# Router gates computed from logits that travel with the gathered token rows, and GpSimd's queue in program order

## The chip, the cores and the metric

The kernel runs on one core of one Trainium2 chip. The metric is the time of one execution in device microseconds. An engine is named PE (TensorE matmuls), PEld (TensorE weight loads), DVE (VectorE), ACT (ScalarE), POOL (GpSimd) or SP (SyncE, which here only issues DMAs).

## What is computed

Three stages run one after another on 3072 tokens of 384 numbers. The first is a complex decaying linear attention, the second a dense gated product, the third a mixture of 8 experts in which each token goes to one expert. The change touches the seam between the second and the third, and the third.

```python
def _moe_ref(x, w_a, w_b, w_out):
    return (x @ w_a) * (x @ w_b) @ w_out

def _moe2_ref(x, w_gate, w1, w2):              # x is [3072, 384], 8 experts
    logits = x @ w_gate
    expert_idx = np.argmax(logits, axis=1)
    logits_shift = logits - logits.max(-1, keepdims=True)
    probs = np.exp(logits_shift)
    probs /= probs.sum(-1, keepdims=True) + 1e-09
    gate_w = probs[np.arange(N), expert_idx]
    for e in range(E):
        mask = expert_idx == e
        h = np.maximum(x[mask] @ w1[e], 0.0)
        out[mask] = gate_w[mask, None] * (h @ w2[e])
```

Because the chosen expert is the one with the largest logit, its gate is 1 divided by the sum of the exponentials of the shifted logits.

## The kernel before

The tokens go through attention and the dense stage in 12 blocks of 256 (j = 0 to 11, two chunks of 128 each). Up to the end of block 10 the order of all instructions on all engines is written out by a planner (`Plan`, with costs and due times). The dense stage of block 11 and the whole expert stage are put together by `merge`, which interleaves lists of steps by position. In that part ACT keeps the order in which the program names its instructions; the order on the other engines, POOL among them, is chosen by the framework's scheduler from its own estimate of times.

At the end of a block's dense stage the PSUM tile `o` of a chunk holds 384 numbers of the token vector and, behind them, 8 router logits (392 columns). `close` copies the 384 into `x2`, and SP stores `x2` to the DRAM table `x2d`. `close` also copies the 8 logits to `lgt`. `route` finds each token's expert from `lgt` (`pick`), its place in that expert's list (`count`, `place`), and scatters the token's number into the table `idtab` (`scatter`, POOL, line 663). `pick` leaves the shifted logits in the resident tile `sh`.

`gates` is called twice: for blocks 0 to 10 while block 11 is in the dense stage, and for block 11 during the first expert slot. It takes the exponential of `sh` on ACT (line 672), sums, adds 1e-9 and inverts on DVE (lines 674 to 676), transposes on PE, and stores one number per token to the DRAM table `gated`.

The expert stage has ten slots, in this order: (0,0), (1,0), (0,BT), (1,BT), then experts 2 to 7. The first four hold 256 tokens each, the others between 372 and 448, in chunks of up to 128 rows. Experts 2, 3 and 4 have a last chunk of 64, 48 or 32 rows of another form. A slot runs through eight steps `up(f)` (nine matmuls into a PSUM tile `h_p`, of which there are two; ACT's Relu at line 780 makes `hH` from it, DVE at line 782 the remainder `hL`) and, two steps behind, `down(f)` (matmuls into `o`, line 803). After the last `up` the next slot's rows are transposed (`turn`, lines 748 to 750). After the last `down` ACT or DVE multiplies `o` by the gate into `ye` (lines 813, 811), and POOL scatters `ye` to the output (line 814).

`fetch` for the slot two later is placed at 0.6 to 0.7 of a slot. SP loads the token numbers `ids` (line 726); then POOL issues one indirect DMA per chunk for the rows `xg` from `x2d` and, behind these, one per chunk for the gates `gt` from `gated` (both line 732).

Of the kernel before, what the change touches and what calls it, by code (L numbers as in the profile page):

```python
# [21 lines left out]
TWO = 2  # L22
# [110 lines left out]
def general(tc, ra, rb, q, k, v, a_re, a_im, w_a, w_b, w_out, w_gate, w1, w2, out, xd, x2d):  # L133
# [27 lines left out]
    with tc.If(ra > 0):  # L161
# [66 lines left out]
        with ExitStack() as ctx:  # L228
# [20 lines left out]
            with tc.For_i(0, NT // C, 1) as i:  # L249
                x = p.tile([128, DM], F32, tag="x", name="g_x")  # L250
                nc.sync.dma_start(out=x, in_=xd.rearrange("(n p) c -> n p c", p=C)[i])
                _, (xH, xL) = rows(p, ps, ident, x)
                o = ps.tile([128, DM], F32, tag="o", name="g_o")
                for f in range(NF):
                    u = []
                    for nm in "ab":
                        t = ps.tile([128, C], F32, tag=nm, name="g_ab")
                        wH, wL = W[nm, f]
                        product(t, [((wH[:, kk * C:(kk + 1) * C], wL[:, kk * C:(kk + 1) * C]), (xH[:, kk], xL[:, kk])) for kk in range(3)])
                        u.append(t)  # L260
# [8 lines left out]
                nc.sync.dma_start(out=x2d[0:NT].rearrange("(n p) c -> n p c", p=C)[i], in_=x2)  # L269
    with tc.If(rb > 0):  # L270
        with ExitStack() as ctx:
# [13 lines left out]
            with tc.For_i(0, NE, 1) as e:  # L285
# [7 lines left out]
                with tc.For_i(0, NT // C, 1) as i:  # L293
                    x = p.tile([128, DM], F32, tag="x", name="g_x")
                    nc.sync.dma_start(out=x, in_=x2d[0:NT].rearrange("(n p) c -> n p c", p=C)[i])
                    xt, (xH, xL) = rows(p, ps, ident, x)
# [153 lines left out]
def body(tc, q, k, v, a_re, a_im, w_a, w_b, w_out, w_gate, w1, w2, out):  # L450
    ins = (q, k, v, a_re, a_im, w_a, w_b, w_out, w_gate, w1, w2)
    with ExitStack() as ctx:
        dram = ctx.enter_context(tc.tile_pool(name="dram", bufs=1, space=bass.MemoryType.DRAM))
        xd = dram.tile([NT, DM], F32, name="xd")
        x2d = dram.tile([NT + 1, DM], F32, name="x2d")
        ra, rb = fast(tc, *ins, out, dram, x2d)
# [4 lines left out]
def fast(tc, q, k, v, a_re, a_im, w_a, w_b, w_out, w_gate, w1, w2, out, dram, x2d):  # L461
# [5 lines left out]
    with ExitStack() as mctx, ExitStack() as ctx:  # L467
# [41 lines left out]
        nc.vector.memset(acc, 0.0)  # L509
        sh = const.tile([128, NT // C, NE], F32, name="sh")  # L510
        gate = const.tile([128, NT // C], F32, name="gate")
        tok = const.tile([128, NT // C], U32, name="tok")
        nc.gpsimd.iota(tok, pattern=[[C, NT // C]], base=0, channel_multiplier=1)
        gated = dram.tile([NT + 1, 1], F32, name="gated")
        idtab = dram.tile([NE * REG, 1], U32, name="idtab")
# [85 lines left out]
        def route(j, late):  # L601
# [3 lines left out]
            def pick():  # L605
# [4 lines left out]
                G["r"], G["oh"] = r, oh  # L610
                sj = sh[:, 2 * j:2 * j + 2]
                eb = ebias.unsqueeze(1).to_broadcast([128, 2, NE])
# [102 lines left out]
        def fetch(e, r0, pool):  # L715
# [4 lines left out]
            def f():  # L720
                ids = pool.tile([128, most], U32, tag="ids" + tag, name="ids", bufs=3)
                same = sum(r == ts[0][1] for _, r, _ in ts)
                for a, b in ((0, same), (same, len(ts))):
                    if a < b:
                        o, r, n = ts[a][0], ts[a][1], b - a
                        nc.sync.dma_start(out=ids[0:r, a:b], in_=idtab.rearrange("(e r) one -> e r one", e=NE)[who[e], r0 + o:r0 + o + n * r].rearrange("(p c) one -> p (c one)", c=n))
                xg = pool.tile([128, most, DM], F32, tag="xg" + tag, name="xg", bufs=2)
                gt = pool.tile([128, most], F32, tag="gt" + tag, name="gt", bufs=3)
                for t, src in ((xg, x2d), (gt, gated)):
                    for c, (_, r, _) in enumerate(ts):  # L730
                        o = t[0:r, c] if t is xg else t[0:r, c:c + 1]
                        nc.gpsimd.indirect_dma_start(o, None, src, bass.IndirectOffsetOnAxis(ap=ids[0:r, c:c + 1], axis=0), bounds_check=NT, oob_is_err=False)  # L732
                SL[e, r0] = [ids, xg, gt, None, None]
            return f
# [18 lines left out]
        def expert(e, r0, pool, after_up):  # L753
# [8 lines left out]
            def up(f):  # L762
                def go():
                    _, _, _, xH, xL = SL[e, r0]
                    t = p_ab.tile([128, n_], F32, tag="ab", name="h_p")
# [22 lines left out]
            def down(f, cs=range(nt)):  # L788
                def go():
# [3 lines left out]
                    for c in cs:  # L793
# [10 lines left out]
                        if f == NH - 1:  # L804
                            y = (mo.tile([128, DM], F32, tag="x2", name="ye", bufs=2) if e < TWO else pool.tile([128, DM], F32, tag="ye", name="ye", bufs=4))
                            if both:
                                nc.vector.tensor_copy(out=y[0:m], in_=G["o", c])
                                nc.gpsimd.dma_start(out=y[0:r], in_=y[r:m], accum_op=ALU.add)
                                nc.gpsimd.tensor_scalar(out=y[0:r], in0=y[0:r], scalar1=gt[0:r, c:c + 1], scalar2=None, op0=ALU.mult)
                            elif c % 2:  # L810
                                nc.vector.tensor_scalar(out=y[0:r], in0=G["o", c], scalar1=gt[0:r, c:c + 1], scalar2=None, op0=ALU.mult)
                            else:
                                nc.scalar.activation(out=y[0:r], in_=G["o", c], func=ACTF.Copy, scale=gt[0:r, c:c + 1])  # L813
                            d = nc.gpsimd.indirect_dma_start(out, bass.IndirectOffsetOnAxis(ap=ids[0:r, c:c + 1], axis=0), y[0:r], None, bounds_check=NT - 1, oob_is_err=False)  # L814
# [187 lines left out]
        def close(j, c):  # L1002

            o = G["o", j, c]
            x2 = mo.tile([128, DM], F32, tag="x2", name="x2", bufs=2)
# [439 lines left out]
        def prefill():  # L1445
            late = x2d[NT - BT:NT].rearrange("(p c) (n t) -> p (c n) t", c=2, t=C)
            fills = [(idtab.rearrange("(p c) one -> p (c one)", p=128), dum, "rx"), (x2d[NT:NT + 1, :].rearrange("a (n t) -> (a n) t", t=C), zeros[0:3, 0:C], "z"), (gated[NT:NT + 1, :], zeros[0:1, 0:1], "z"),
                     (gated[NT - BT:NT].rearrange("(a t) one -> a (t one)", a=1), zeros[0:1], "z")]
            fills += [(late[:, 2 * i:2 * i + 2].rearrange("p n t -> p (n t)"), zeros, "z") for i in range(3)]
            for n, (o, i, x) in enumerate(fills):  # L1450
# [133 lines left out]
```

## Time and profile before

| | before |
|---|---|
| median of 3 runs | 912.55 us (911.75 to 915.97) |
| the profiled execution, its own time | 914.04 us |
| its span, first to last instruction | 912.2 us |
| PE busy | 850.9 us (93%) |
| DVE, ACT, POOL busy | 557.2, 477.2, 352.5 us |

The profile is of one execution. Times in it count from the first instruction. The expert stage begins at about 645.7 us, when the last matmul of the dense stage is issued. An engine's busy share does not by itself say what an operation is worth; what the engine waited for in that stretch does. The start of a PE record is when the engine took the matmul up, and its end is modelled. A wait named "issue" ended with nothing that the profile shows.

### The profile page before, as it was taken

What the parts mean: (1) busy time and instruction counts of PE and PEld (TensorE: products, weight loads), DVE (VectorE), ACT (ScalarE), POOL (GpSimd) and SP (SyncE); (2) the same over time, 40 slices, a digit from 0 to 9 for tenths busy, and PEclk for the clock granted to TensorE, in tenths of its full rate; (3) what the DMA queues carried; (4) which work ended last, traced back from release to release, by engine and by line L of the source; (5) the groups of instructions that cost most, each with busy time, mean ns of one, the idle gap of its engine ahead of it and who ended that gap; (6) DMA issues with size and microseconds to landing.
All of it is one profiled execution on the core that took longest, in us unless ns stands there. A gap on an engine that the chain in (4) does not pass through costs nothing.

```text
span 912.2 us, 20675 instructions
## 1 busy us (share of the span) xinstructions
PE 850.9 (93%) x8188; PEld 816.7 (90%) x8188; DVE 557.2 (61%) x1217; ACT 477.2 (52%) x887; POOL 352.5 (39%) x338
## 2 busy tenths in 40 slices
PE   0399999999999999999999999999995999999995
PEld 0387899999999999999999999999995999999995
DVE  6999997683838475666757593445731545455540
ACT  6487887574656474655655552224521534344430
POOL 2341441414454545363544444204163343444311
PEclk9999999999999999999999999999997999999998
DMA  9999964433242452627274524123341544454511
GB/s 254 276 279 236 244 142 124 103 90 100 69 96 81 109 170 65 200 60 217 63 208 69 167 59 145 36 88 122 105 153 35 160 133 138 147 161 129 164 51 25
DMA packets 134379, 120.17 MB, mean 132 GB/s; under 512 B 37284, under 2 KB 128820, under 8 KB 134271
## 3 DMA queue, kind: packets, MB, share of 16 engines
q1 hardware_dynamic: 121151, 100.51, 39.3%
q0 software_dynamic: 11392, 17.43, 8.3%
q8 instruction: 67, 1.10, 0.5%
q10 hardware_dynamic: 1728, 0.79, 0.4%
q14 instruction: 41, 0.34, 0.2%
HBM read 82.42 MB, written 10.56 MB: 102 GB/s over the span
## 4 chain that ended last, share of the span: by engine, by line
PE 72%; issue 13%; DMA 5%; POOL 5%; DVE 3%; SPq 1%; ACT 0%; POOLq 0%; DVEq 0%; ACTq 0%
PE ab_p L957 31%; PE o L1000 16%; PE h_p L771 4%; PE sc_p L1335 4%; PE y_p L1374 4%; PE o L803 4%; PE ab_p L965 3%; POOL gt L732 2%; POOL out_dram L814 2%; PE o L971 2%; PE kv_p L1394 2%; DMA out_dram<-ye,ids 1%; PE kn_p L1344 1%; DMA v<-in_v_dram 1%; DMA ids<-idtab 1%
## 5 line engine op out<-in xcount | busy, mean ns | idle before, releaser
L957 PE MATMUL ab_p<-xH,wL 128*128 128x256 f32 x792 | 220.9, 279 | 0.0
L957 PEld LDWEIGHTS ab_p<-xH,wL 128*128 128x128 f32 x792 | 148.8, 188 | 0.0
L991 POOL TENSOR_TENSOR gL<-g,gH 128x256 fp32r<-128x256 f32 x96 | 80.3, 838 | 171.4 <-ACT gH L987 166.9
L980 ACT COPY g<-ab_p 128x256 f32<-128x256 f32 x132 | 48.8, 370 | 133.6 <-PE ab_p L957 124.3
L983 DVE TENSOR_TENSOR g<-g,ab_p 128x256 f32<-128x256 f32 (+1 forms) x148 | 60.7, 410 | 90.3 <-ACT g L980 87.0
L957 PE MATMUL ab_p<-xH,waH 128*128 128x256 f32 x396 | 113.7, 287 | 0.0
L957 PE MATMUL ab_p<-xL,waH 128*128 128x256 f32 x396 | 111.1, 281 | 0.0
L957 PE MATMUL ab_p<-xH,wbH 128*128 128x256 f32 x396 | 110.6, 279 | 0.0
L957 PE MATMUL ab_p<-xL,wbH 128*128 128x256 f32 x396 | 110.4, 279 | 0.0
L1000 PE MATMUL o<-woH,gH 128*128 128x392 f32 x264 | 96.4, 365 | 0.0
L1000 PE MATMUL o<-wL,gH 128*128 128x392 f32 x264 | 90.3, 342 | 0.0
L1000 PE MATMUL o<-woH,gL 128*128 128x392 f32 x264 | 90.2, 342 | 0.0
L771 PE MATMUL h_p<-sH,w1H 128*128 128x256 f32 (+5 forms) x240 | 78.2, 326 | 11.2 <-issue 10.2
L803 PE MATMUL o<-w2H,h 128*128 128x384 f32 (+3 forms) x312 | 86.2, 340 | 0.0
L771 PE MATMUL h_p<-sL,w1H 128*128 128x256 f32 (+5 forms) x240 | 77.4, 323 | 0.0
L771 PE MATMUL h_p<-sH,w1L 128*128 128x256 f32 (+5 forms) x240 | 77.4, 322 | 0.0
L987 ACT ACTIVATE gH<-g 128x256 fp32r<-128x256 f32 x132 | 54.5, 413 | 40.3 <-DVE g L983 36.7
L957 PEld LDWEIGHTS ab_p<-xH,waH 128*128 128x128 f32 x396 | 74.5, 188 | 0.9 <-issue 0.2
L957 PEld LDWEIGHTS ab_p<-xL,waH 128*128 128x128 f32 x396 | 74.6, 188 | 0.4
L957 PEld LDWEIGHTS ab_p<-xL,wbH 128*128 128x128 f32 x396 | 74.5, 188 | 0.0
L957 PEld LDWEIGHTS ab_p<-xH,wbH 128*128 128x128 f32 x396 | 74.4, 188 | 0.0
L814 POOL DMA_INDIRECT out_dram<-ye,ids x29 | 30.2, 1040 | 92.9 <-ACT ye L813 84.2
(210 smaller groups left out, 2162.8 us busy)
## 6 DMA issues: line engine op xcount, KB each, us to landing
raw<-in_moe_w_dram SPq DMA_DIRECT2D x64, 384.0 KB
q<-in_q_dram SPq DMA_DIRECT2D x24, 192.0 KB
v<-in_v_dram SPq DMA_DIRECT2D x24, 192.0 KB
raw<-in_moe_w_a_dram SPq DMA_DIRECT2D x12, 384.0 KB
raw<-in_moe_w_b_dram SPq DMA_DIRECT2D x12, 384.0 KB
raw<-in_moe_w_out_dram SPq DMA_DIRECT2D x12, 384.0 KB
wL<-a POOLq DMA_DIRECT2D x24, 192.0 KB
x2d<-x SPq DMA_DIRECT2D x24, 192.0 KB
```

The costliest lines, as they stand in the source:

```text
L771: nc.tensor.matmul(out=t, lhsT=lh[:, o:o + 128], rhs=rh[:, kk], start=n == 0, stop=n == 8)
L803: nc.tensor.matmul(out=G["o", c], lhsT=lh, rhs=rh, start=f == 0 and n == 0, stop=f == NH - 1 and n == len(ops) - 1)
L814: d = nc.gpsimd.indirect_dma_start(out, bass.IndirectOffsetOnAxis(ap=ids[0:r, c:c + 1], axis=0), y[0:r], None, bounds_check=NT - 1, oob_is ...
L957: nc.tensor.matmul(out=t[:, i], lhsT=lh[:, kk * 128:(kk + 1) * 128], rhs=rh[:, kk], start=n == 0, stop=n == 8)
L965: nc.tensor.matmul(out=t[:, i], lhsT=A32[nm, f][:, kk * 128:(kk + 1) * 128], rhs=xT["F", 0][:, kk, cs[0]:cs[0] + len(cs)].rearrange("p c t ...
L980: nc.scalar.copy(out=G["g", j, f], in_=G["ab", j, f][:, 0])
L983: nc.vector.tensor_tensor(out=G["g", j, f], in0=G["g", j, f], in1=G["ab", j, f][:, 1], op=ALU.mult)
L987: nc.scalar.activation(out=G["H", j, f], in_=G["g", j, f], func=ACTF.Copy)
L991: eng.tensor_tensor(out=G["L", j, f], in0=G["g", j, f], in1=G["H", j, f].bitcast(F32), op=ALU.subtract)
L1000: nc.tensor.matmul(out=G["o", j, c], lhsT=lh[:, c * C:(c + 1) * C], rhs=rh, start=f == first and n == 0, stop=f == last and n == 2)
L1335: nc.tensor.matmul(out=S["p", hg][:, h], lhsT=pq["k", j][:, hg * 4 + h, c, :], rhs=pq["q", j][:, hg * 4 + h, c, 0:C], start=True, stop=True)
L1374: nc.tensor.matmul(out=t[q4 * 32:q4 * 32 + 32, kk], lhsT=a, rhs=b, start=f0, stop=f1)
```

## The change

The logits are stored and gathered with the token vector: rows of `x2d` grow from 384 to 392 numbers, `close` copies all 392 columns, and `xg` holds 392 per row. The table `gated`, the tiles `sh` and `gate`, both calls of the old `gates`, and all gathers of `gt` go. In each slot, after `up(2)`, a new `gates` has ACT copy the 8 logits of each gathered row out of `xg` into `ex`, and DVE take their largest and subtract it; after `up(5)`, `gated` has ACT take the exponential and DVE sum, add 1e-9 and invert into `gt`. Slots whose last chunk has another size do this in two parts. In the part put together by `merge`, POOL too now keeps the order in which the program names its instructions.

```diff
-        x2d = dram.tile([NT + 1, DM], F32, name="x2d")
+        x2d = dram.tile([NT + 1, DM + NE], F32, name="x2d")
...
-                sj = sh[:, 2 * j:2 * j + 2]
+                sj = mo.tile([128, 2, NE], F32, tag="sj", name="sj")
...
-        def gates(t0, t1):
-
-            def f():
-                n = t1 - t0
-                ex = mo.tile([128, NT // C, NE], F32, tag="rx", name="ex")
-                nc.scalar.activation(out=ex[:, 0:n], in_=sh[:, t0:t1], func=ACTF.Exp)
-                gs = gate[:, t0:t1].unsqueeze(2)
-                nc.vector.tensor_reduce(out=gs, in_=ex[:, 0:n], axis=AX.X, op=ALU.add)
-                nc.vector.tensor_scalar(out=gs, in0=gs, scalar1=1e-9, scalar2=None, op0=ALU.add)
-                nc.vector.reciprocal(out=gs, in_=gs)
-                t = p_sc.tile([n, C], F32, tag="sc", name="gt_p")
-                nc.tensor.transpose(t, gate[:, t0:t1], ident)
-                gT = mo.tile([NT // C, C], F32, tag="gT", name="gT")
-                nc.vector.tensor_copy(out=gT[0:n], in_=t)
-                nc.sync.dma_start(out=gated[t0 * C:t1 * C].rearrange("(n t) one -> n (t one)", t=C), in_=gT[0:n])
-            return f
...
-                xg = pool.tile([128, most, DM], F32, tag="xg" + tag, name="xg", bufs=2)
-                gt = pool.tile([128, most], F32, tag="gt" + tag, name="gt", bufs=3)
-                for t, src in ((xg, x2d), (gt, gated)):
-                    for c, (_, r, _) in enumerate(ts):
-                        o = t[0:r, c] if t is xg else t[0:r, c:c + 1]
-                        nc.gpsimd.indirect_dma_start(o, None, src, ...)
+                xg = pool.tile([128, most, DM + NE], F32, tag="xg" + tag, name="xg", bufs=2)
+                for c, (_, r, _) in enumerate(ts):
+                    nc.gpsimd.indirect_dma_start(xg[0:r, c], None, x2d, ...)
...
+        def gates(e, r0, pool):
...
+                gt = S_[2] = pool.tile([128, most, 1], F32, tag="gt" + tag, name="gt", bufs=2)
+                ex = pool.tile([128, most, NE], F32, tag="ex" + tag, name="ex", bufs=1)
+                same = sum(r == ts[0][1] for _, r, _ in ts)
+                parts = [(a, b, ts[a][1]) for a, b in ((0, same), (same, len(ts))) if a < b]
+                for a, b, r in parts:
+                    nc.scalar.copy(out=ex[0:r, a:b], in_=S_[1][0:r, a:b, DM:DM + NE])
+                for a, b, r in parts:
+                    x, g = ex[0:r, a:b], gt[0:r, a:b]
+                    nc.vector.tensor_reduce(out=g, in_=x, axis=AX.X, op=ALU.max)
+                    nc.vector.tensor_tensor(out=x, in0=x, in1=g.to_broadcast([r, b - a, NE]), op=ALU.subtract)
...
+        def gated(e, r0):
...
+                for a, b, r in parts:
+                    nc.scalar.activation(out=ex[0:r, a:b], in_=ex[0:r, a:b], func=ACTF.Exp)
+                for a, b, r in parts:
+                    g = gt[0:r, a:b]
+                    nc.vector.tensor_reduce(out=g, in_=ex[0:r, a:b], axis=AX.X, op=ALU.add)
+                    nc.vector.tensor_scalar(out=g, in0=g, scalar1=1e-9, scalar2=None, op0=ALU.add)
+                    nc.vector.reciprocal(out=g, in_=g)
...
                 st.append((0.98, up(f)))
+                if f == 2:
+                    st.append((0.1, gates(e, r0, pool if e >= TWO else xp)))
+                if f == 5:
+                    st.append((0.1, gated(e, r0)))
...
-                nc.scalar.copy(out=x2, in_=o[:, 0:DM])
+                nc.scalar.copy(out=x2, in_=o)
             else:
-                nc.vector.tensor_copy(out=x2, in_=o[:, 0:DM])
+                nc.vector.tensor_copy(out=x2, in_=o)
...
-        mctx.enter_context(tc.manual_schedule(engines={mybir.EngineType.Activation}))
-        NL = 2 * (NB - 1)
+        mctx.enter_context(tc.manual_schedule(engines={mybir.EngineType.Activation, mybir.EngineType.Pool}))
...
-              (0.45, 0.5, [(1, gates(0, NL)), (1, fetch(0, 0, xp)), (1, fetch(1, 0, xp))]))
+              (0.45, 0.5, [(1, fetch(0, 0, xp)), (1, fetch(1, 0, xp))]))
...
-                st.append((0.02, 0.5, route(NB - 1, True)[0] + [(0.2, gates(NL, 2 * NB)), (0.1, check)]))
+                st.append((0.02, 0.5, route(NB - 1, True)[0] + [(0.1, check)]))
```

## Rows read from the trace of the kernel before

**Rows 1.** The page, granted TensorE clock in 40 slices, tenths of full speed.

```profile
PEclk9999999999999999999999999999997999999998
```

**Rows 2.** Windows by slot: length, busy (count) of each engine, clock, DMA share, GB/s.

```profile
682.00:712.10 30.10, 19.91 (x129) 19.70 (x128) 5.07 (x12) 5.02 (x12) 8.94 (x9) 0.83 0.12 37
...
764.30:795.00 30.70, 30.70 (x172) 29.57 (x171) 15.76 (x30) 12.45 (x23) 13.14 (x13) 1.00 0.47 146
```

**Rows 3.** Windows around trains of POOL's DMAs, columns PE, PEld, DVE, ACT, POOL.

```profile
662.80:671.30 8.50, 8.50 (x64) 8.39 (x63) 4.15 (x7) 3.58 (x7) 6.84 (x6) 1.00 0.38 129
...
684.20:694.40 10.20, 0.06 (x1) 0.06 (x1) 1.04 (x2) 0.96 (x2) 7.07 (x8) 0.71 0.23 75
694.40:698.80 4.40, 4.40 (x18) 4.40 (x19) 0.85 (x2) 0.77 (x2) 0.00 (x0) 0.50 0.02 7
...
744.70:755.40 10.70, 10.70 (x59) 10.35 (x58) 4.81 (x9) 4.57 (x7) 8.43 (x8) 1.00 0.54 172
```

**Rows 4.** Timeline of PE: start, duration, instruction, [idle before <- what ended it].

```profile
681.17 0.34 PE L803 MATMUL o<-w2H,hL 128*128 128x384 f32 x1
...
683.87 0.28 PE L771 MATMUL h_p<-sH,w1L 128*128 128x256 f32 x1
694.35 0.58 PE L771 MATMUL h_p<-sH,w1H 128*128 128x256 f32 x1 [10.19 <-issue]
...
711.17 0.33 PE L803 MATMUL o<-w2H,hL 128*128 128x384 f32 x1
...
730.78 0.34 PE L803 MATMUL o<-w2H,hL 128*128 128x384 f32 x1
...
736.25 0.45 PE L771 MATMUL h_p<-sH,w1H 128*128 128x448 f32 x1 [0.97 <-DVE h L784]
```

**Rows 5.** Timeline of ACT, the same columns.

```profile
685.60 0.58 ACT L813 ACTIVATE ye<-o,gt 128x384 f32<-128x384 f32 x1 [5.28 <-PE h_p L771]
693.45 0.38 ACT L780 ACTIVATE hH<-h_p 128x256 fp32r<-128x256 f32 x1 [7.27 <-remote]
...
711.55 0.58 ACT L813 ACTIVATE ye<-o,gt 128x384 f32<-128x384 f32 x1 [2.09 <-PE o L803]
...
734.37 0.58 ACT L813 ACTIVATE ye<-o,gt 128x384 f32<-128x384 f32 x1 [3.24 <-PE h_p L771]
```

**Rows 6.** Timeline of POOL, the same columns.

```profile
675.46 1.05 POOL L732 DMA_INDIRECT xg<-x2d,ids  x1 [4.21 <-DMA ids<-idtab]
...
680.73 1.00 POOL L732 DMA_INDIRECT xg<-x2d,ids  x1 [0.30 <-issue]
...
692.41 1.00 POOL L814 DMA_INDIRECT out_dram<-ye,ids  x1 [0.30 <-issue]
...
732.25 0.94 POOL L732 DMA_INDIRECT gt<-gated,ids  x1 [0.30 <-issue]
```

**Rows 7.** POOL by line: count, busy us, mean ns, idle before it.

```profile
L732 POOL DMA_INDIRECT gt<-gated,ids x29 | 33.1, 1142 | 11.5 <-issue 8.5 <-DMA gated<-gT 3.0
```

**Rows 8.** ACT and DVE by line, the small operations.

```profile
L915 ACT COPY a<-wg_p 128x8 f32<-128x8 f32 x12 | 1.9, 161 | 1.5 <-PE wg_p L912 1.5
L672 ACT ACT_TABLE_LOAD x1 | 1.3, 1283 | 0.0
...
L672 ACT ACTIVATE ex<-sh 128x16 f32<-128x16 f32 x1 | 0.2, 207 | 0.0
...
L613 DVE TENSOR_REDUCE rm<-lgt 128x2 f32<-128x16 f32 x1 | 0.2, 170 | 0.0
```

**Rows 9.** The chain that ended last: start us, us, what.

```profile
684.15 10.19 issue
...
699.75 1.05 PE o L803 x6
700.80 1.07 PE h_p L771 x9
...
785.73 1.76 POOL gt L732
```

More of the change, by code (lines that the diff above doesn't have):

```diff
@@ L268, in general @@
                 nc.scalar.copy(out=x2, in_=o)
-                nc.sync.dma_start(out=x2d[0:NT].rearrange("(n p) c -> n p c", p=C)[i], in_=x2)
+                nc.sync.dma_start(out=x2d[0:NT, 0:DM].rearrange("(n p) c -> n p c", p=C)[i], in_=x2)
     with tc.If(rb > 0):
@@ L294, in general @@
                     x = p.tile([128, DM], F32, tag="x", name="g_x")
-                    nc.sync.dma_start(out=x, in_=x2d[0:NT].rearrange("(n p) c -> n p c", p=C)[i])
+                    nc.sync.dma_start(out=x, in_=x2d[0:NT, 0:DM].rearrange("(n p) c -> n p c", p=C)[i])
                     xt, (xH, xL) = rows(p, ps, ident, x)
@@ L509, in fast @@
         nc.vector.memset(acc, 0.0)
-        sh = const.tile([128, NT // C, NE], F32, name="sh")
-        gate = const.tile([128, NT // C], F32, name="gate")
         tok = const.tile([128, NT // C], U32, name="tok")
         nc.gpsimd.iota(tok, pattern=[[C, NT // C]], base=0, channel_multiplier=1)
-        gated = dram.tile([NT + 1, 1], F32, name="gated")
         idtab = dram.tile([NE * REG, 1], U32, name="idtab")
@@ L726, in f @@
                         nc.sync.dma_start(out=ids[0:r, a:b], in_=idtab.rearrange("(e r) one -> e r one", e=NE)[who[e], r0 + o:r0 + o + n * r].rearrange("(p c) one -> p (c one)", c=n))
-                xg = pool.tile([128, most, DM], F32, tag="xg" + tag, name="xg", bufs=2)
-                gt = pool.tile([128, most], F32, tag="gt" + tag, name="gt", bufs=3)
-                for t, src in ((xg, x2d), (gt, gated)):
-                    for c, (_, r, _) in enumerate(ts):
-                        o = t[0:r, c] if t is xg else t[0:r, c:c + 1]
-                        nc.gpsimd.indirect_dma_start(o, None, src, bass.IndirectOffsetOnAxis(ap=ids[0:r, c:c + 1], axis=0), bounds_check=NT, oob_is_err=False)
@@ L733, in f @@
-                SL[e, r0] = [ids, xg, gt, None, None]
+                xg = pool.tile([128, most, DM + NE], F32, tag="xg" + tag, name="xg", bufs=2)
+                for c, (_, r, _) in enumerate(ts):
+                    nc.gpsimd.indirect_dma_start(xg[0:r, c], None, x2d, bass.IndirectOffsetOnAxis(ap=ids[0:r, c:c + 1], axis=0), bounds_check=NT, oob_is_err=False)
+                SL[e, r0] = [ids, xg, None, None, None]
+            return f
+        def gates(e, r0, pool):
+            ts = shape(e)
+            most, tag = (2, "2") if e < TWO else (4, "4")
+            def f():
+                S_ = SL[e, r0]
+                gt = S_[2] = pool.tile([128, most, 1], F32, tag="gt" + tag, name="gt", bufs=2)
[8 more added lines that the diff above has]
+                    nc.vector.tensor_tensor(out=x, in0=x, in1=g.to_broadcast([r, b - a, NE]), op=ALU.subtract)
+                S_.append((ex, parts))
+            return f
@@ new lines, in gated, with f @@
+        def gated(e, r0):
+            def f():
+                gt, (ex, parts) = SL[e, r0][2], SL[e, r0][5]
+                for a, b, r in parts:
[5 more added lines that the diff above has]
+                    nc.vector.reciprocal(out=g, in_=g)
@@ L763, in go @@
                 def go():
-                    _, _, _, xH, xL = SL[e, r0]
+                    xH, xL = SL[e, r0][3:5]
                     t = p_ab.tile([128, n_], F32, tag="ab", name="h_p")
@@ L804, in go @@
                         if f == NH - 1:
-                            y = (mo.tile([128, DM], F32, tag="x2", name="ye", bufs=2) if e < TWO else pool.tile([128, DM], F32, tag="ye", name="ye", bufs=4))
+                            y = (mo.tile([128, DM + NE], F32, tag="x2", name="ye", bufs=2)[:, 0:DM] if e < TWO else pool.tile([128, DM], F32, tag="ye", name="ye", bufs=4))
                             if both:
@@ L808, in go @@
                                 nc.gpsimd.dma_start(out=y[0:r], in_=y[r:m], accum_op=ALU.add)
-                                nc.gpsimd.tensor_scalar(out=y[0:r], in0=y[0:r], scalar1=gt[0:r, c:c + 1], scalar2=None, op0=ALU.mult)
+                                nc.gpsimd.tensor_scalar(out=y[0:r], in0=y[0:r], scalar1=gt[0:r, c], scalar2=None, op0=ALU.mult)
                             elif c % 2:
-                                nc.vector.tensor_scalar(out=y[0:r], in0=G["o", c], scalar1=gt[0:r, c:c + 1], scalar2=None, op0=ALU.mult)
+                                nc.vector.tensor_scalar(out=y[0:r], in0=G["o", c], scalar1=gt[0:r, c], scalar2=None, op0=ALU.mult)
                             else:
-                                nc.scalar.activation(out=y[0:r], in_=G["o", c], func=ACTF.Copy, scale=gt[0:r, c:c + 1])
+                                nc.scalar.activation(out=y[0:r], in_=G["o", c], func=ACTF.Copy, scale=gt[0:r, c])
                             d = nc.gpsimd.indirect_dma_start(out, bass.IndirectOffsetOnAxis(ap=ids[0:r, c:c + 1], axis=0), y[0:r], None, bounds_check=NT - 1, oob_is_err=False)
@@ L1004, in close @@
             o = G["o", j, c]
-            x2 = mo.tile([128, DM], F32, tag="x2", name="x2", bufs=2)
+            x2 = mo.tile([128, DM + NE], F32, tag="x2", name="x2", bufs=2)
             if c == 0:
                 lgt[j] = mo.tile([128, 2, NE], F32, tag="lgt", name="lgt", bufs=2)
-                nc.scalar.copy(out=x2, in_=o[:, 0:DM])
+                nc.scalar.copy(out=x2, in_=o)
             else:
-                nc.vector.tensor_copy(out=x2, in_=o[:, 0:DM])
+                nc.vector.tensor_copy(out=x2, in_=o)
             nc.vector.tensor_copy(out=lgt[j][:, c], in_=o[:, DM:DM + NE])
@@ L1445, in prefill @@
         def prefill():
[L1446 to L1449, printed above, removed]
+            late = x2d[NT - BT:NT].rearrange("(p c) n -> p (c n)", c=2)
+            fills = [(idtab.rearrange("(p c) one -> p (c one)", p=128), dum, "rx"), (x2d[NT:NT + 1, :].rearrange("a (n t) -> (a n) t", t=(DM + NE) // 4), zeros[0:4, 0:(DM + NE) // 4], "z")]
+            fills += [(late[:, a:min(a + BT, 2 * (DM + NE))], zeros[:, 0:min(BT, 2 * (DM + NE) - a)], "z") for a in range(0, 2 * (DM + NE), BT)]
             for n, (o, i, x) in enumerate(fills):
```

## The prediction

> **What bounds the kernel now.** I read the page first: PE is busy 93% of the span, so what counts is where PE is not full. The clock line of the page shows one slice inside the kernel below nine tenths [rows 1], at 680 to 700 us, in the expert stage. The windows by slot put a size to it: slot (0,BT), 682.0 to 712.1 us, is 30.10 us long and holds 19.91 us of PE work, at a mean clock of 0.83; a later slot, 764.3 to 795.0, is full, 30.70 of 30.70 [rows 2]. The chain that ended last shows the hole as one piece of 10.19 us called "issue" [rows 9], and PE's timeline puts it between a matmul of 683.87 and one of 694.35 [rows 4]. In the 4.40 us behind the hole PE runs at a granted clock of 0.50, which is the lower of its two levels (1.2 GHz), after 10.2 us with nothing to do [rows 3]. So 10.19 us are lost, and half of 4.40, or 2.20.
>
> Who makes PE wait? It is about to start `up(2)` of the slot, and there are only two `h_p` tiles, so it needs ACT's Relu of `up(0)`, then DVE's remainder. ACT's Relu starts at 693.45, although the matmuls of `up(0)` and `up(1)` were all taken up by 683.87 [rows 4, 5]. Before it ACT did `ye` of slot (1,0) at 685.60, and the last matmul that this needs ends by its record at 681.17 + 0.34 = 681.51 [rows 4, 5]. ACT was idle in between and started 4.09 us late. At the end of slot (0,BT) the same pair stands at 711.17 + 0.33 = 711.50 and 711.55, late by 0.05 [rows 4, 5]. At the end of (1,BT) it is 730.78 + 0.34 = 731.12 and 734.37, late by 3.25, and PE then waits 0.97 us for DVE at 736.25 [rows 4, 5].
>
> So at two slot ends news of finished matmuls reaches ACT late. What do they have in common? POOL's timeline: from 675.46 to 692.41 it issues fourteen indirect DMAs one behind another, 1.3 us each (680.73 to 692.41 is nine of them), and the Relu of 693.45 comes 0.04 us after the last one ends at 693.41 [rows 5, 6]. In program order that train would be two pieces. The scheduler took the fetch of slot (2,0), four gathers of rows and four of gates from 680.73 on, ahead of the two scatters of slot (1,0). At the second late end eight gathers ran until 732.25 + 0.94 = 733.19 [rows 6]. At the punctual end of 711.55 POOL had been idle since 693.41. My reading is that PE's completions are held up while POOL builds descriptors for long, and that the hold grows along a train. The reading has exceptions: six DMAs in a row at 662.8 to 671.3 left PE full, 8.50 of 8.50, and so did eight at 744.7 to 755.4, 10.70 of 10.70 [rows 3].
>
> A page bears on this. The Trainium skill, Perfetto Trace Analysis, in its summary of the profiler window per engine type, says that for TensorE a record runs to an estimated end and that the true end and the semaphore's travel are hidden. The trace agrees in so far as a record ended at 681.51 and its consumer began at 685.60. By that page the matmuls themselves may have run late for a reason of their own; then the hole is not POOL's and stays. That is rival B.
>
> **The change part by part.**
>
> *Gathers of `gt` go.* That is 29 issues of 1.14 us, 33.1 us of POOL [rows 7]. POOL is not what PE waits for from 744 us on: the chain does run through it there, as at 785.73 [rows 9], but PE has no gap in that stretch [rows 2], so I count the 33.1 us as nothing by themselves. What they do is shorten the trains: fourteen loses six, the eight at 722 to 733 lose four.
>
> *POOL in program order.* The order differs from before in one place only, the fetch of (2,0). In the new order POOL issues two gathers for (1,BT), waits for `ye` of (1,0) at about 682, issues two scatters, then four gathers, done near 690. The rows of (2,0) are first needed about 35 us later, so waiting costs them nothing. In all other slots the fetch already stood ahead of the scatters.
>
> *Gain.* If the hold goes, the hole (10.19), the half-speed stretch (2.20) and the wait at 736.25 (0.97) go: 13.36 us. What can come back: the scatters of (1,0) and the gathers of (2,0) make a train of six, about 7.8 us, in the first steps of (0,BT). From below it costs nothing, as the train of six in rows 3. From above, a hold as long as the one found six us into the long train, 4.09. PE bears a good part of that: from the end of an `up` to the `up` that needs its tile there are 1.05 + 1.07 + 1.05 = 3.17 us of other matmuls [rows 9], of which ACT's Relu (0.38, rows 5) and a DVE operation on as many elements take about 0.85, so some 2.3 us are spare. 4.09 less 2.3 is 1.8. I take the middle, 0.9, as neither row is nearer.
>
> *New gate work.* Ten slots, of which three have two parts: 13 parts. Each part is a copy (0.161) and an exponential (0.207) on ACT, and five operations of 0.17 on DVE [rows 8]: 13 x 0.37 = 4.8 us on ACT and 13 x 0.85 = 11.1 us on DVE. Both are half idle in a slot, 12.45 and 15.76 us busy of 30.70 [rows 2]. The cover is the 2.3 us spare: a Relu that comes 0.2 us late, or a remainder 0.85 late, is inside it. Without cover it would be 11.1 us. The exponential's table load (1.283, rows 8) moves from the dense stage to the first slot, once, and is inside the spare too. I allow 0.4 us for the spot where DVE is fullest. Behind ACT's copy in its queue stands only the next Relu; its rows landed before the slot began, so it adds no wait of its own.
>
> *Edits at nothing.* The old gate work (two exponentials, two transposes, two stores) was spread over a full PE and gave no gap; taking it out is worth 0 to 0.6. Copies of 392 instead of 384 columns, 24 of them, cost each 2% of half a microsecond, beside PE's work. Rows of 1568 bytes instead of 1536 make each gather and store 2% larger; the gathers land several us before they are read. The zero fills at 150 us are one DMA fewer, on SP. The tail behind the last matmul is not touched.
>
> *Sum.* The profiled execution took 914.04 us. 914.04 - 13.36 + 0.9 + 0.4 = 901.98. The median of the runs is 1.49 lower than the profiled one, so 900.5.
>
> **Rivals.**
>
> *B: the hole stays.* What stalls PE at 684 is not POOL's train, as the two trains without a hold suggest, or the new train of six does the same. Then at most the 0.97 at 736 is won and 0.4 paid: 912. For it: those two exceptions, and that rows cannot show what keeps a completion back. Against it: at the two late ends POOL was at work on a train, at the punctual one it was not.
>
> *D: half a hole.* The train of six holds completions by as much as 8 us; the idle stretch is 5 us and PE still falls to 1.2 GHz for a while: 905 to 910. For it: the hold rose along the long train, from 4.09 us at 685.60 to more at 693.45.
>
> *C: slower.* The gate operations stand on DVE ahead of a remainder that PE needs, in the slots where DVE also splits weights. The point from which it decides is a delay beyond 2.3 us: the two-part slots put 1.7 us on DVE in two lumps, beside a weight split of about 1 us, so a lump has to meet two splits. If half of the 11.1 us comes onto the path and the hole stays, 912.55 + 5.5 = 918; with the hole gone it would still be under 908. For it: PE has waited once for DVE in this stage [rows 4]. Against it: DVE's half-idle slots [rows 2].
>
> **How the numbers follow.** My forecast, the hole gone, has 0.66 and 897.5 to 905.5 of its own; D 0.08; B 0.18, at 910.5 to 914; C 0.08, 917 and more. About 0.5% is what can be told from no change, here 4.6 us: below 908.0 is faster, above 917.1 slower. Faster takes the forecast and most of D, 0.73; within, B and the rest of D, 0.19; slower C, 0.08. The range runs from 897.5, which is the sum without what comes back and with 1.7 us for the old gate work and the second train, to 914.0, the end of B.
>
> **What would show it.** Right: no gap above 3 us on PE between 645 and 900 us, no granted clock of 0.50 before the tail, `ye` of slots (1,0) and (1,BT) within 0.3 us of their last matmul's record, POOL's scatters of (1,0) ahead of the gathers of (2,0). Gate work right: PE's waits for DVE in the stage stay below 2 us in sum. Wrong: a gap of 5 us or more in the first steps of (0,BT) though POOL's train is short, or late starts of ACT while POOL is idle.

## The result, and the profile after

| | before | changed |
|---|---|---|
| median | 913.59 us (4 runs, 911.75 to 915.97) | 901.99 us (4 runs, 899.94 to 906.47) |
| ratio | | 0.9868, 95% interval 0.9834 to 0.9903 |
| the profiled execution | 914.04 us, span 912.2 | 900.33 us, span 898.6 |

Faster by 1.3%, as forecast; 901.99 against 900.5, inside the range. The experiments show a condition that the forecast did not know: what the change takes away is there on some chips only.

The page's clock line of the changed kernel, to be laid beside [rows 1], has lost its dip at 680 to 700 us:

```profile
PEclk9999999999999999999999999999999999999998
```

The window of slot (0,BT) is 17.70 us long instead of 30.10, PE is busy in all of it and the clock is 1.00; the later slot of [rows 2], 764.3 to 795.0, is as full as before. Columns as there:

```profile
681.60:699.30 17.70, 17.70 (x127) 17.57 (x127) 5.71 (x16) 4.63 (x14) 6.05 (x6) 1.00 0.22 67
...
764.30:795.00 30.70, 30.70 (x174) 29.58 (x173) 16.60 (x41) 13.12 (x27) 9.43 (x9) 1.00 0.48 145
```

What PE waited for from 645 to 904 us, longest first; the 10.2 and the 1.0 of before are gone:

```profile
PE tn_p L758 <- issue: 0.7, 1, 0.7
PE tn_p L758 <- DVE sL L760: 0.3, 1, 0.3
```

POOL's timeline shows the new order: two gathers, a wait for `ye`, then six DMAs in a row, of which these are the first, the third and the last:

```profile
682.13 1.02 POOL L824 DMA_INDIRECT out_dram<-ye,ids  x1 [3.93 <-ACT ye L823]
...
684.76 1.05 POOL L709 DMA_INDIRECT xg<-x2d,ids  x1 [0.30 <-issue]
...
688.73 0.97 POOL L709 DMA_INDIRECT xg<-x2d,ids  x1 [0.31 <-issue]
```

ACT's timeline beside it: `ye` of slot (1,0) is punctual, 0.04 us behind its last matmul's record (and so is that of (1,BT)), but at the end of the train and just behind it two Relus come late:

```profile
681.27 0.58 ACT L823 ACTIVATE ye<-o,gt 128x384 f32<-128x384 f32 x1 [2.09 <-PE o L813]
...
687.93 0.39 ACT L790 ACTIVATE hH<-h_p 128x256 fp32r<-128x256 f32 x1 [2.28 <-PE h_p L781]
690.84 0.38 ACT L790 ACTIVATE hH<-h_p 128x256 fp32r<-128x256 f32 x1 [2.53 <-PE h_p L781]
```

The second one's last matmul, by PE's timeline:

```profile
689.08 0.28 PE L781 MATMUL h_p<-sH,w1L 128*128 128x256 f32 x1
```

By its record it ends at 689.08 + 0.28 = 689.36, so the Relu starts 1.48 us late; the one before it starts 0.68 us late in the same way, and 0.04 is usual. This is what is called a **hold** from here on: a consumer starts late although its producer's record has ended. The train of six still holds, and PE's spare time covers it.

Executions begin the expert stage at different times: its first matmul starts at 645.38 us here and at 649.74 in another profile of the same kernel. So the experiments are also compared by the **stretch**: from that matmul's start to the end of the span. Before it is 912.24 - 645.74 = 266.5 us, here 898.62 - 645.38 = 253.2.

### The profile page after: what moved, and what is told of

Same layout as the page of the kernel before. It is cut to its first block, busy times and chain, and to the rows that moved or that the text cites. A ratio compares the mean times of both kernels' runs of the same rounds, so it can differ in the third digit from the quotient of the medians.

```text
span 898.6 us, 20668 instructions
## 1 busy us (share of the span) xinstructions
PE 850.5 (95%) x8186; PEld 816.1 (91%) x8186; DVE 561.0 (62%) x1274; ACT 479.9 (53%) x911; POOL 320.2 (36%) x309
## 4 chain that ended last, share of the span: by engine, by line
PE 73%; issue 13%; DMA 4%; DVE 4%; POOL 4%; SPq 1%; ACT 0%; POOLq 0%; DVEq 0%
PE ab_p L971 31%; PE o L1014 16%; PE sc_p L1349 5%; PE y_p L1388 4%; PE h_p L781 4%; PE o L813 3%; PE ab_p L979 3%; PE o L985 2%; POOL out_dram L824 2%; PE kv_p L1408 2%; PE kn_p L1358 1%; DMA out_dram<-ye,ids 1%; POOL xg L709 1%; DMA q<-in_q_dram 1%; DMA ids<-idtab 1%
```

## The experiments

Four groups ran, each on a chip of its own, with the kernel before timed beside them. A chip whose traces show holds is called a holding chip.

| chip | kernel before there, median | runs of it |
|---|---|---|
| first (order_alone to no_gate_work) | 899.74 us (897.04 to 904.11) | 35 |
| second (before_again to train_late) | 913.93 us (911.7 to 919.33) | 25 |
| third (order and gates again) | 899.22 us (897.08 to 903.06) | 19 |
| fourth (first_gates_late, order_third) | 914.57 us (910.69 to 918.48) | 15 |

The same kernel before takes 14 to 15 us more on two of the chips.

**Order alone** (first, third and fourth chip). The kernel before with one line:

```diff
-tc.manual_schedule(engines={mybir.EngineType.Activation})
+tc.manual_schedule(engines={mybir.EngineType.Activation, mybir.EngineType.Pool})
```

> The kernel before with one edit: POOL in program order. All 29 gathers of gates stay. POOL then issues two gathers of rows and two of gates for slot (1,BT), waits for ye of slot (1,0), and issues ten DMAs in a row (two scatters, four rows, four gates), about 13 us from 682 on. Theory A (completions of matmuls are held while POOL issues a long train, more the longer it is): the hold now falls late in the train, over the first steps of slot (0,BT), and is as large as at the tenth place of the long train; a PE gap of 2 to 8 us between 684 and 700, and the 1 us gap near 736 stays: 904 to 911 us. Rival O (what costs is only that the scatters and with them ye stand behind the fetch; order is the whole gain): no gap above 1 us before 730, 901 to 903. Rival B (the gap is PE's own and has nothing to do with POOL): the gap of 10 stays at about 684, 912 to 914.

> The kernel before with POOL in program order and nothing else, again, in the hope of a chip on which completions are held (on the first chip no completion was held in any of four traces and the kernel before took 899.7 us; on the next the kernel before took 913.9, the changed one 904.1, and 14 gathers in a row cost 15.5 us early and 5 us late). POOL issues ten DMAs in a row behind ye of slot (1,0). Theory A on such a chip: six in a row held completions by 0.7 and 1.5 us, which PE's spare time hid, fourteen by 11 to 16; ten hold them by 3 to 9, PE has a gap of 1 to 7 us between 686 and 702, and the wait near 736 stays: 3 to 9 us below the kernel before, with 264 to 270 us... from the first matmul of the stage to the end of the program, where the kernel before has 266.5 and the changed one 253.3, so 255 to 263. Rival O (order is the whole gain): 252 to 254 for that stretch. On a chip that holds nothing: 252, equal to the kernel before.

> The kernel before with POOL in program order and nothing else, on another chip; the two chips that it has run on hold no completion (0 of 551 each time, the kernel before at 899.2 and 899.7). If this chip holds them (kernel before 912 or more): theory A, ten DMAs in a row behind ye of slot (1,0) hold completions by 3 to 9 us, 1 to 7 us of it reach PE, 255 to 263 us from the first expert matmul to the end, where the kernel before has 266; rival O (order is the whole gain): 252 to 254. If it holds none: 252, and the same time as the kernel before.

Measured: 899.89 us and 899.04 us on the first and third chip, ratio 0.9995 (0.9981 to 1.0009; 0.9981 to 1.0010), stretch 252.2 and 252.0. On the fourth 909.55, ratio 0.9945 (0.9921 to 0.9969), stretch 263.0. Theory A's gap of 2 to 8 us did not come on the first and the third chip. POOL issues the same ten DMAs in a row each time. This is the end of that train on the third chip, by POOL's timeline, and ACT's timeline beside it:

```profile
694.82 0.99 POOL L732 DMA_INDIRECT gt<-gated,ids  x1 [0.30 <-issue]
696.12 0.96 POOL L732 DMA_INDIRECT gt<-gated,ids  x1 [0.30 <-issue]
```

```profile
691.52 0.39 ACT L780 ACTIVATE hH<-h_p 128x256 fp32r<-128x256 f32 x1 [1.73 <-PE h_p L771]
693.63 0.39 ACT L780 ACTIVATE hH<-h_p 128x256 fp32r<-128x256 f32 x1 [1.73 <-PE h_p L771]
695.75 0.38 ACT L780 ACTIVATE hH<-h_p 128x256 fp32r<-128x256 f32 x1 [1.73 <-PE h_p L771]
```

And on the fourth chip, the same two views, PE's last matmul for the late Relu, and what PE waited for in the stage:

```profile
693.54 1.00 POOL L732 DMA_INDIRECT gt<-gated,ids  x1 [0.31 <-issue]
694.84 0.96 POOL L732 DMA_INDIRECT gt<-gated,ids  x1 [0.30 <-issue]
```

```profile
688.85 0.39 ACT L780 ACTIVATE hH<-h_p 128x256 fp32r<-128x256 f32 x1 [2.45 <-PE h_p L771]
694.59 0.38 ACT L780 ACTIVATE hH<-h_p 128x256 fp32r<-128x256 f32 x1 [5.35 <-remote]
```

```profile
689.90 0.28 PE L771 MATMUL h_p<-sH,w1L 128*128 128x256 f32 x1
```

```profile
PE h_p L771 <- DVE h L784: 3.4, 1, 3.4
PE h_p L771 <- DVE hL L782: 2.7, 2, 2.1
```

The same kernel, the same train; on the third chip the Relus start 2.1 us apart all through it, on the fourth one starts 694.59 - 690.18 = 4.41 us late. So the train holds on one chip and not at all on the other. Where it does, order alone brings 0.55%, 5.0 us of 914.57. What is left there stands for the most part further on: behind eight gathers and two scatters PE waits 3.4 us, and from 729.0 to 736.5 us its mean clock is 0.54, which costs it about 3 us more. Rival O (order is the whole gain) falls, and B falls with it: moving POOL's DMAs moved the hole.

**Gates alone** (first and third chip). The changed kernel with the line above taken back, so that the scheduler again puts the fetch of (2,0) ahead of the scatters of (1,0).

> The changed kernel with one edit undone: POOL's order is the scheduler's again. It takes the four gathers of slot (2,0) ahead of the two scatters of slot (1,0) as in the kernel before, so POOL issues eight DMAs in a row (six gathers, two scatters) from about 675.5 to 686; no gathers of gates anywhere. Theory A: the end of slot (1,0) at 681.5 lies at the fifth or sixth place of the train, where the long train had already held a completion by 4 us, so ye is 1 to 4 us late and PE loses 0 to 3 us: 901 to 905. Rival O (order is the whole gain): the hole comes back to 7 us or more, 908 to 913. Rival G (the removed gathers are the whole gain): no gap, 900 to 902.

> The changed kernel with the scheduler's order on POOL, again, on the same chip as the run above. Eight DMAs in a row, six gathers ahead of the two scatters of slot (1,0). Theory A on a chip that holds completions: the end of slot (1,0) meets the fifth of them, held by 0.5 to 3 us, and the steps behind meet the last three; PE loses 0 to 4 us there, 253 to 258 us from the first matmul of the stage to the end. Rival O (order is the whole gain): 262 or more. On a chip that holds nothing: 253 to 257, as the 256.7 of the first time, of which 2.6 were a wait for a weight split at 671.

Measured: 901.33 and 900.80 us, ratios 1.0016 (0.9998 to 1.0035) and 1.0019 (1.0004 to 1.0033), stretches 256.7 and 254.2. On these chips there was no hold to take away, so the runs price the rest of the change: some 1.6 us slower, the first interval just including no change. One new wait shows, by ACT's and then PE's timeline on the first chip:

```profile
668.80 0.84 ACT L677 ACTIVATE w1H<-raw 128x768 fp32r<-128x768 f32 x1 [3.09 <-DMA raw<-in_moe_w_dram]
669.55 0.64 ACT L790 ACTIVATE hH<-h_p 128x256 fp32r<-128x256 f32 x2
```

```profile
671.02 0.39 PE L781 MATMUL h_p<-sH,w1H 128*128 128x256 f32 x1 [2.44 <-DVE hL L792]
```

A weight load lands late, ACT's weight split waits for it with the Relus queued behind, and PE waits 2.44 us (1.49 on the third chip). On the first chip its mean clock then is 0.72 from 671 to 677 us; the two together make that stretch the longer one. Run no_gate_work shows where that starts. Whether the removed gathers alone would do on a holding chip was not measured.

**Gathers put back** (first chip). The changed kernel, and behind each fetch:

```diff
+                for c, (_, r, _) in enumerate(ts):
+                    nc.gpsimd.indirect_dma_start(gd[0:r, c:c + 1], None, gated_d, ...)
```

> The changed kernel with 29 gathers of one number per row put back behind the gathers of rows, from a table of zeros, read by nothing; the gates still come from the logits. POOL's order is the program's. The train behind ye of slot (1,0) has ten DMAs again, as in the order alone. Theory A: a PE gap of 2 to 8 us between 684 and 700 and some wait near 731 to 736, 904 to 911, within 2 us of the run with the order alone. Rival O: no gap, 901 to 903.

Measured: 901.52 us, ratio 1.0010 (0.9994 to 1.0026), stretch 253.5; the one wait of PE, 0.8 us at 672.59, stands ahead of the train. In this execution the train is not ten but fourteen DMAs long, of which these are the first and the last by POOL's timeline, as many as in the train behind the hole of the kernel before:

```profile
682.84 1.05 POOL L710 DMA_INDIRECT xg<-x2d,ids  x1 [4.29 <-ACT hH L794]
699.91 0.96 POOL L713 DMA_INDIRECT gd<-gated_d,ids  x1 [0.30 <-issue]
```

No Relu in it starts more than 0.1 us late. So theory A as the forecast has it, that such a train always holds, is wrong on this chip. 29 gathers more cost nothing that shows there, as the forecast counted them.

**No gate work** (first chip). `gates` and `gated` are not called and the gate is a constant 1.

> The changed kernel with the gate work of the slots left out: no copies of logits, no exponentials, no sums, the gate is the constant 1, so the output lacks the gates. POOL as in the changed kernel. What it gains is the price of the new gate work. My sum has 0.4 us for it and 2.3 us of spare time that hides the rest: 0 to 1 us faster than the changed kernel, 901 to 902. Rival C (the 11 us on DVE or the 4.8 us on ACT reach the path): 3 us or more faster, below 899.

Measured: 901.96 us, ratio 1.0021 (1.0004 to 1.0038): no faster than the two runs with gate work beside it, so by the times gate work costs nothing that can be told. But in its profile PE waits for nothing in the stage and the stretch is 251.3, the shortest of all; the stage began at 648.28, late. A place where gate work can cost is read from the traces. DVE's timeline of the changed kernel has the token places of block 11 (`posu`, which the scatter to `idtab` waits for) 9.04 us after the stage's first matmul, as the new reduction and subtraction and a weight split moved ahead of the routing:

```profile
650.20 0.17 DVE L728 TENSOR_REDUCE gt<-ex 128x2 f32<-128x16 f32 x1
650.27 0.95 DVE L678 TENSOR_TENSOR w1L<-raw,w1H 128x768 fp32r<-128x768 f32 x1
651.14 0.17 DVE L729 TENSOR_TENSOR ex<-ex,gt 128x16 f32<-128x16 f32 x1
...
654.42 0.14 DVE L647 CAST posu<-pos 128x2 uint32<-128x2 f32 x1
```

In the kernel before it is 652.67 - 645.74 = 6.93 us and without gate work 655.38 - 648.28 = 7.10:

```profile
652.67 0.15 DVE L650 CAST posu<-pos 128x2 uint32<-128x2 f32 x1
```

Behind `posu` stand the scatter, then SP's load of token numbers, and in SP's queue the next weights. SP's timeline of the changed kernel:

```profile
660.57 0.35 SPq L706 DMA_DIRECT2D ids<-idtab  x1
...
661.80 2.62 SPq L674 DMA_DIRECT2D raw<-in_moe_w_dram  x1
```

The load of token numbers is issued 15.19 us into the stage; in the kernel before it goes out at 659.00, which is 13.26. PE's wait at the start of slot (1,0) is 0 to 2.5 us in the traces with gate work and 0 without. That this wait comes from the gate work by way of SP's queue is an argument from these traces; the runs' times do not resolve it.

**Before and changed kernel again** (second chip), unchanged.

> The kernel before, unchanged, profiled beside the runs of this group. In the first group of experiments the kernel before took 899.74 us in 35 runs on that chip, against 912 to 916 on the chip of the forecast, and putting POOL in program order changed nothing there. Theory A as the forecast has it (the train of fourteen always holds completions) demands the gap of 10 us at about 684 and a time near 912. Rival H (the hold comes with the chip or the way the program lies in its memory, the train is only what it needs beside that): no gap above 1 us, the same fourteen DMAs in a row, and about 900 us.

> The changed kernel, unchanged, on the same chip as the kernel before. Theory A: 900 to 903, faster than the kernel before by 11 to 13 us. Rival H: where the kernel before has no hole the change is worth nothing or costs its gate work: 900 to 902 beside 900.

Measured: 914.43 us and 904.05, ratio of the changed one 0.9875 (0.9836 to 0.9913), stretches 265.9 and 253.3. What PE waited for in the kernel before, a hole at the place of the forecast's trace, a little shorter:

```profile
PE h_p L771 <- issue: 7.9, 1, 7.9
PE h_p L771 <- DVE h L784: 2.2, 1, 2.2
```

The result repeats on a chip that holds: 9.9 us between the two medians there.

**Two trains of fourteen** (second chip). The changed kernel with 14 gathers of one number per row in a row, at half of slot (0,BT), or at a quarter of slot (5,0):

```diff
+            if (e, r) == (0, BT):      # the other run: (5, 0), 0.25
+                st.append((0.5, 0.5 + 0.1, [(1, dummies(e, r))]))
```

> The changed kernel with 14 gathers of one number per row (from a table of zeros, read by nothing) issued one behind another at half of slot (0,BT), in front of the fetch, about 18 us of POOL and more with the fetch behind. Theory A: completions are held up to several us from about the fourth on, PE gaps of 3 to 12 us between 697 and 720 and a granted clock of 0.50 for some us: 905 to 915. Rival H where the chip shows no hold: no gap above 1 us and no change beyond 1 us; the fetch of slot (3,0) comes 18 us later, 10 us or more before its rows are needed.

> The same 14 gathers at a quarter of slot (5,0), where slots are full and the trains of the kernel before left PE full. Theory A: a gap of 3 to 12 us in slot (5,0), 905 to 915. Rival S (trains hold completions only in the first slots, where weights are not split): no gap there, within 1 us of the changed kernel, while the early train has one. Rival H: neither has one.

Measured: 919.52 us and 909.03, against 904.05 of the changed kernel on that chip: 15.5 and 5.0 us for gathers that nobody reads, the first more than theory A gave. The windows around the early train, which with the scatters before it and the fetch behind it runs from 689.32 to 715.12:

```profile
690.00:699.00 9.00, 9.00 (x67) 8.87 (x66) 1.98 (x6) 1.63 (x5) 6.86 (x8) 1.00 0.13 45
699.00:716.00 17.00, 3.82 (x21) 2.65 (x19) 1.00 (x4) 0.87 (x3) 12.47 (x13) 0.76 0.16 39
716.00:722.00 6.00, 6.00 (x26) 6.00 (x27) 2.13 (x6) 1.64 (x4) 0.00 (x0) 0.55 0.04 11
```

PE is full from 690 to 699 us, does 3.82 us of work in the next 17, and runs at about half clock behind them. The timelines of POOL, ACT and PE up to the train's end:

```profile
714.15 0.97 POOL L711 DMA_INDIRECT xg<-x2d,ids  x1 [0.30 <-issue]
```

```profile
700.88 0.38 ACT L799 ACTIVATE hH<-h_p 128x256 fp32r<-128x256 f32 x1 [5.35 <-issue]
714.97 0.38 ACT L799 ACTIVATE hH<-h_p 128x256 fp32r<-128x256 f32 x1 [13.71 <-remote]
```

```profile
703.69 0.43 PE L822 MATMUL o<-w2H,hH 128*128 128x384 f32 x1
705.09 0.33 PE L822 MATMUL o<-w2L,hH 128*128 128x384 f32 x1 [0.96 <-issue]
706.48 0.33 PE L822 MATMUL o<-w2H,hL 128*128 128x384 f32 x1 [1.07 <-issue]
715.87 0.58 PE L790 MATMUL h_p<-sH,w1H 128*128 128x256 f32 x1 [9.05 <-issue]
```

The hold was made at will, and here it lasts up to the train's last DMA. PE also slows down inside one group of matmuls, whose operands were all there: they are 1.4 us apart (703.69, 705.09, 706.48), with a weight load between each two, where 0.17 is usual. The late train, in a full slot, brings a gap of 3.23 us, 17 us after its first gather, and one of 1.4 behind its end:

```profile
840.62 0.55 PE L767 MATMUL tn_p<-ident,xg 128*128 128x128 f32 x3 [3.23 <-issue]
850.92 0.44 PE L790 MATMUL h_p<-sH,w1H 128*128 128x384 f32 x1 [1.41 <-DVE h L801]
```

Rival S falls too: full slots are not spared by a train as long as this one.

**First slot's gates later** (fourth chip). The changed kernel with

```diff
-                if f == 2:
+                if f == (5 if (e, r0) == (0, 0) else 2):
                     st.append((0.1, gates(...)))
-                if f == 5:
+                if f == (6 if (e, r0) == (0, 0) else 5):
                     st.append((0.1, gated(e, r0)))
```

> The changed kernel with the gate work of the first slot moved: slot (0,0) takes its logits out and subtracts after its sixth up instead of the third, and takes the exponential after the seventh; all other slots as in the changed kernel. Theory R (the gate work costs where its DVE operations stand ahead of the routing of block 11 in the first slot: the token places come 2 us later after the stage begins, 9.04 against 7.00, the load of token numbers 1.9 us later, the weight loads behind it on SP late, ACT's weight split ahead of a Relu late, and PE waits 0.6 to 2.7 us at the start of slot (1,0)): the token places at 7.3 us or less, no PE wait above 0.5 us in slot (1,0), 251.3 to 252.6 us from the first expert matmul to the end of the program, against 253.2 and 253.3 of the changed kernel and 251.3 without gate work; 899 to 900.5 where the kernel before takes 899.5. Rival D (the price is DVE's and ACT's extra work in all ten slots): 252.9 to 253.5, and 901 to 902 there.

Measured: 902.92 us, ratio 0.9874 (0.9848 to 0.9901), the same as the changed kernel's 0.9868 and 0.9875. `posu` is back at 654.01 - 646.89 = 7.12 us and the wait in slot (1,0) is 0.4, as R says; but the changed kernel itself has 0 there in one profile and 0.6 in another. The stretch of 255.8 is outside what R gave. The load of token numbers still goes out only 14.83 us into the stage, since POOL's two scatters to `idtab` take 1.75 and 1.77 us, where the kernel before needs 1.02 and 0.97. And PE waits 0.8 and 0.7 us in the transposes at 717 to 719, just behind a train of four, after which its mean clock is 0.66 from 719 to 724 us. The scatters by POOL's timeline, and the longest waits of the stage:

```profile
654.46 1.75 POOL L660 DMA_INDIRECT idtab<-tok,posu  x1 [22.44 <-DVE posu L647]
658.56 1.77 POOL L660 DMA_INDIRECT idtab<-tok,posu  x1 [2.35 <-DMA idtab<-tok,posu]
```

```profile
PE tn_p L758 <- DVE sL L760: 1.0, 2, 0.7
PE tn_p L758 <- issue: 0.8, 1, 0.8
PE h_p L781 <- DVE hL L792: 0.4, 1, 0.4
```

So what delays `posu` is shown; that the wait and the price hang on it is not, and there is no gain. No version was found that beats the changed kernel on a holding chip.

## Why the prediction was right, step by step

**The hole is POOL's train** (0.66): shown on holding chips, by taking the train apart (the changed kernel), by moving it (order alone, hole moved and smaller), and by adding one (15.5 us). How much of the gain is the order's and how much the removed gathers' is known in part: order alone brings 5.0 us, the gathers alone were not measured on a holding chip. What the forecast lacked is that the hold comes and goes from one group of runs to another: on two of four chips trains of ten, and on one of them a train of fourteen, hold nothing, and the kernel before is as fast there as with its order mended. That the result, too, was taken where completions are held was luck. Each chip was used in one group only, so a chip cannot be told from whatever else a group shares. (In program order the gathers of the first two fetches also change places, rows and gates, which the forecast overlooked; no wait stands there.) The two exceptions that rival B rested on need no cause of PE's own: a train of six holds by 0.7 and 1.5 us on a holding chip too, which does not reach PE. That eight in a row at 745 to 755 left PE full while eight at 722 to 733 did not stays unexplained.

**Gain, 13.36.** The hole, the half clock and the wait at 736 are all gone: the slot shrank by 30.10 - 17.70 = 12.40 (10.19 + 2.20 were counted), and 0.97 on top.

**What comes back, 0.9.** Too much: the train of six held two Relus by 0.68 and 1.48 us, and PE lost nothing there, the lower bound.

**Gate work, 0.4.** Its size is not resolved. On the first chip, from the stage's first matmul to PE's last, it is 242.79 us without gate work and 244.04 with it and the gathers put back, 1.25 us in single executions; by the medians it is nothing. So 0.4 may be too small. The place that the traces point to is another than the forecast's: not a remainder that comes late in a two-part slot but the routing of block 11 in the first slot, with SP's queue behind it. The forecast named what stands behind ACT's copy, but not what stands behind DVE's reduction.

**Edits at nothing.** The tail was to stay; from PE's last matmul to the end it went from 9.44 to 8.68 us. It goes with the 29 gathers: it is 9.44 to 9.50 in the six traces that have them, also where they were put back into the changed kernel, and 8.39 to 9.07 in the eight that do not. Why was not tested.

**The sum.** Of the span's 912.24 - 898.62 = 13.62 us, 0.36 are an earlier start of the stage, 0.76 the shorter tail, and 12.50 lie between. So of the 13.36 there was 0.86 for what comes back, gate work and all else that differs, where the forecast put 0.9 + 0.4. The profiled 900.33 against 901.98 is thus in part luck: 1.1 of the 1.65 us are tail and start, for which the forecast had nothing.

**Rivals.** B and D did not happen on a chip that holds. B's time, no change, is about what a chip without the hold would give, by another mechanism: there was no hole. The changed kernel itself was not timed on such a chip; the four runs nearest to it, gates alone twice, gathers put back and no gate work, took 1.6 to 2.2 us more than the kernel before. C's mechanism (gate work ahead of something that PE needs) is possible at 0 to 2.5 us, far under the 5.5 it was given.

**A rival that no run tests.** Each timed run here has a span and a clock, so all of them were recorded while they ran, and the recording itself may have a part in the hold. Two things speak for it. The traces of holding chips lack completions of DMAs: for the weight loads the page gives no time from issue to landing in all eight traces with holds, the forecast's two among them, and gives it in all six others. These are its lines in the kernel before and in order alone on the first chip; the last number is that time:

```profile
raw<-in_moe_w_dram SPq DMA_DIRECT2D x64, 384.0 KB
```

```profile
raw<-in_moe_w_dram SPq DMA_DIRECT2D x64, 384.0 KB, 3.5
```

And PE, where it is held, is slowed inside a group for which it needed nothing more. Whether a chip holds when nothing is recorded stays open, and with it what the gain is then.

The Trainium skill, Perfetto Trace Analysis, summary of the profiler window per engine type, has a TensorE record run to an estimated end, with the true end and the semaphore's travel hidden. The traces agree so far: by its records PE took up its work on time while ACT started 4.41 us late (order alone, fourth chip). Whether the matmuls or only the news of them were late, no run here shows; the slow matmuls of one group speak for PE itself being held.

## What to carry to other kernels

When a consumer starts late although its producer's record has long ended, look at what all other engines did in that stretch, and test it by adding more of the suspect, not only by taking it away: 14 idle gathers settled in one run what the first two traces left open. Keep POOL's indirect DMAs in short groups, and let a scatter that frees something go before a fetch that has time. Time both kernels on more than one chip before a gain is believed: here it was 1.3% on holding chips, and on the others the kernel before had no hole to lose.

## What the hardware showed that was not expected

- The hold behind POOL's indirect DMAs goes with the chip (or with what else a group of runs shares). With ten in a row a Relu was on time on one chip and 4.41 us late on another; the kernel before took 899.2 and 899.7 us on two chips, 913.9 and 914.6 on two others.
- On a holding chip it grows along the train. 5.8 us after the train's start a Relu was 0.68 us late in the changed kernel, 0.78 with order alone and 0.70 in the early train; 11.6 us after it, 4.41 and 4.32. In the early train, 689 to 715 us, ACT was then idle for 13.71 us and came back as the train ended.
- A load issue on SP behind the token numbers took 2.62 us instead of 0.37 in the changed kernel, 2.51 to 3.43 in six other profiles with gate work, and 0.37 without gate work and with the first slot's gates later; its cause was not found.
